# Gated attention on one core: where TensorE's early code is aligned, the rings of the first loads, and the last column block

## The chip, the core and the metric

The kernel runs on one core of a Trainium2 chip. A core has five engines with an instruction stream each: TensorE (PE), which multiplies 128x128 weight tiles with up to 512 columns; VectorE (DVE); ScalarE (ACT); GpSimd (POOL); and SyncE (SP), which here only issues DMA transfers. ACT and POOL can issue transfers as well; each issuing engine has a ring of its own. Engines wait for each other through semaphores. The metric is the device time of one execution in microseconds (us).

## What is computed

```python
xn = layernorm(x)                                # x: 2048 x 640
q  = xn @ wq                                     # 32 heads of 128
s  = concat(softmax(q k^T / sqrt(128)) v) @ wo   # the last 512 keys of the cache
g  = silu(relu(xn @ w1 + b1)**2 @ w2 + b2)       # 640 -> 1728 -> 640
return x + s * g
```

All in float32. A matmul operand is split in a high and a low part (`hi`, `lo` in the names), and one product becomes three matmuls: hi x hi, hi x lo, lo x hi.

## The kernel before

The 2048 rows of x are four tiles of 512 columns once transposed (D on the partitions, five blocks of 128). The work is laid out by hand in one long stream for each engine; `Ordered` (line 69) keeps the engines' instructions in the order in which they are written.

1. **The head**, `ln_first` (226). The first tile's x comes as four blocks of 128 rows. Block 0 is halved between SP's and ACT's rings; blocks 1 and 3 are issued by SP, block 2 by ACT (lines 239 to 243). In the meantime TensorE turns the identity `WARM` times (`pw`, 250). DVE takes the statistics block by block, ACT and POOL make the root, ACT scales blocks 0 and 1, DVE blocks 2 and 3, and TensorE turns them by transposes (`px`). ACT and DVE split the result into `xT`, hi and lo.
2. **The MLP of tiles 0 to 2**, `mlp_step` (471), one call a step over `steps`, 14 chunks of the hidden dimension for each tile. Step n does the up-projection of chunk n (`up`, 414, psum `ph`; relu, square and split follow on ACT, POOL and DVE) and then the down-projection of chunk n - 1 (`down`, 442, five psums `py`). A whole chunk is 15 matmuls up and 15 down; the chunk of 64 rows has 10 and 10. Weights are loaded and split on the way in tile 0. In one step of each tile a transpose of the next tile's layer norm statistics stands behind the up-projection (`ln_rows`, 176).
3. **Attention**, 128 units in a fixed period, planned by times in a list `plan` and sorted (lines 986 to 1181): scores, maximum, exponent, values, output projection into `acc`. The MLP of the last tile is spread over the end of it (`late_up`, `late_down`).
4. **The end.** `late_down` fills the psums `ly` one column block after the other, and `late_gate` (925) finishes each: ACT's silu into a tile `lsg` in SBUF, DVE's product with the attention's result `acc`, DVE's sum with x (`lx`), and a store issued by SP. The last block, d = 4, is done in two halves of 256 columns: both silus, then product, sum and store of the first half, then those of the second.

`pe.addr_align(BLOCK, slot)` fills TensorE's instruction stream with NOPs until the next instruction stands at `slot`, counted modulo `BLOCK` = 256 instructions. It is called at the beginning of the warm-up with `LEAD_SLOT` = 88 (line 249), and five times in each attention unit (`align`, 1021), at `FIRST_SLOT` = 188 plus 128 for odd units plus an offset of `SLOTS`. Between line 249 and the first unit there is none.

Of the kernel before, what the change touches and what calls it, by code (L numbers as in the profile page):

```python
# [8 lines left out]
F32 = mybir.dt.float32  # L9
F32R = mybir.dt.float32r  # L10
AF = mybir.ActivationFunctionType
ALU = mybir.AluOpType
AX = mybir.AxisListType

P = 128
NT = 512
EPS = 1e-5
WARM = 40
BLOCK = 256
FIRST_SLOT = 188  # L20
SLOTS = (0, 11, 22, 33, 42)
LEAD_SLOT = 88


@with_exitstack
def kernel(
# [20 lines left out]
    DC = D // P  # L47
# [3 lines left out]
    LN_AT = {t: (3, 7) if t == LATE else (5, 9) for t in range(1, NTILE)}  # L51
    SCALE = DH**-0.5
    G = 2
    HALF = 2
# [8 lines left out]
    b1_sb, b2_sb = b_sb[:, :FC], b_sb[:, FC : FC + DC]  # L63
    chunks = [(f0, min(P, F - f0)) for f0 in range(0, F, P)]
# [4 lines left out]
    class Ordered:  # L69
# [13 lines left out]
    pe, dve, act, pool, sp = (  # L83
        Ordered(e) for e in (nc.tensor, nc.vector, nc.scalar, nc.gpsimd, nc.sync)
    )
# [8 lines left out]
    def raw(ap):  # L94
        return ap.bitcast(F32)
# [39 lines left out]
    def ln_tile(t, b):  # L135
        tag = "stage" if b < 2 else "mr"
        return xp.tile([P, D], F32, tag=tag, name=f"xb{t}_{b}")
# [3 lines left out]
    def ln_load(t):  # L141
        mv = xp.tile([P, 4, NB], F32, tag="mv", name=f"mv{t}")[:, :2, :]
        sc = xp.tile([P, 3, NB], F32, tag="sc", name=f"sc{t}")
        xn = []
        for b in range(NB):
            xb = ln_tile(t, b)
            r0 = t * NT + b * P
            nc.sync.dma_start(xb, x[r0 : r0 + P, :])
            xn.append(xb)
        LS[t] = mv, sc, xn  # L150

    def ln_block(t, b):
        mv, sc, xn = LS[t]
        st = xp.tile([P, 2, 6], F32, tag="st", name=f"st{t}_{b}", bufs=4)
        hd = D // 2
        for i in range(2):
            dve.bn_stats(st[:, i, :], xn[b][:, i * hd : (i + 1) * hd])
        dve.bn_aggr(mv[:, :, b], st)

    def ln_var(t):  # L160
        mv, sc, xn = LS[t]
        dve.tensor_scalar(sc[:, 0, :], mv[:, 1, :], EPS, None, op0=ALU.add)
        nc.scalar.activation(sc[:, 1, :], sc[:, 0, :], AF.Sqrt)

    def ln_root(t):
        mv, sc, xn = LS.pop(t)
        var, sd, y = (sc[:, i, :] for i in range(3))
        r = mv[:, 1, :]
        dve.reciprocal(y, sd)
        dve.tensor_tensor(r, y, y, op=ALU.mult)  # L170
        dve.tensor_tensor(r, r, var, op=ALU.mult)
        dve.tensor_scalar(r, r, -0.5, 1.5, op0=ALU.mult, op1=ALU.add)
        dve.tensor_tensor(r, r, y, op=ALU.mult)
        return mv
# [21 lines left out]
    def ln_chunk(t, bc, xs, c):  # L196
        xc = xp.tile([P, D], F32, tag="stage", name=f"xc{t}_{c}")[:, :NT]
        nc.sync.dma_start(xc, xT[c * P : (c + 1) * P, t * NT : (t + 1) * NT])
        dve.tensor_tensor(xc, xc, bc[0], op=ALU.subtract)
        nc.vector.tensor_tensor(xc, xc, bc[1], op=ALU.mult)  # L200
        nc.scalar.activation(xs[0][:, c, :], xc, AF.Copy)
        nc.vector.tensor_tensor(xs[1][:, c, :], xc, raw(xs[0][:, c, :]), op=ALU.subtract)
# [23 lines left out]
    def ln_first():  # L226
# [3 lines left out]
        n = NB // 2  # L230
# [7 lines left out]
        xn = [ln_tile(0, b) for b in range(NB)]  # L238
        for i, q in enumerate((sp, act)):
            js = slice(i * hd, (i + 1) * hd)  # L240
            q.dma_start(xn[0][:, js], x[:P, js])
        for b in range(1, NB):
            (sp if b % 2 else act).dma_start(xn[b], x[b * P : (b + 1) * P, :])
        act.activation(warm, warm, AF.Sqrt)
        br = xp.tile([P, P], F32, tag="br", name="br", bufs=1)
        dve.memset(br, 0.0)
        BR.append(br)
        pw = psx.tile([P, NT], F32, tag="x", name="pw")
        pe.addr_align(BLOCK, LEAD_SLOT)
        for _ in range(WARM):  # L250
            pe.transpose(pw[:, :P], ident, ident)
        pts = [ps_y.tile([P, NT], F32, tag="py", name=f"px0_{c}") for c in range(DC)]
        xs = [
            xp.tile([P, DC, NT], F32R, tag=f"xT{i}", name=f"xT0_{i}", bufs=1) for i in range(2)
        ]
# [59 lines left out]
        for cs in (range(2), range(2, DC)):  # L315
            js = slice(cs[0] * P, (cs[-1] + 1) * P)
            for b in range(n, NB):
                m, q = mv[:, 0, b : b + 1], mv[:, 1, b : b + 1]
# [17 lines left out]
    def spill(t, xs, cs=slice(0, DC)):  # L336
        for i in range(2):
            pool.dma_start(xT_d[t][i][:, cs, :], raw(xs[i])[:, cs, :])

    def load_part(f, k, held=False):  # L340
        f0, n = chunks[f]
        if f % 3 and f < 9:
            if k == 0:
                BOTH[f] = keep.tile([P, 2, D], F32, tag="acc", name=f"wr{f}", bufs=2)
            w = BOTH[f][:, k, :]
        else:
            w = xp.tile([P, D], F32, tag="stw", name=f"w{k + 1}r{f}", bufs=2)
            if held:
                dve.memset(w[:, :1], 0.0)
        if k == 0:  # L350
            w = w.rearrange("p (c n) -> p c n", n=P)[:, :, :n]
            sp.dma_start(w, w1[:, f0 : f0 + n].rearrange("(c p) f -> p c f", p=P))
        else:
            for i in range(0, P, n):
                sp.dma_start(w[i : i + n, :], w2[f0 : f0 + n, :])
        PRE[f, k] = w
# [14 lines left out]
    def split_w(f, k):  # L371
        if f < FC:
            split_hi(f, PRE[f, k], k)
            split_lo(f, PRE[f, k], k, dve)
            if 9 <= f < FC - 1:
                load_part(f + 1, k)
# [81 lines left out]
    steps = [(t, f) for t in range(LATE) for f in range(FC)]  # L458
    XS, HS, PY, LN = {0: xs_next}, {}, {}, {}

    def gate(t, tiles):
        for d in range(DC):
# [5 lines left out]
            )  # L468
            nc.gpsimd.dma_start(g_d[t][:, d, :], sg)

    def mlp_step(n):
        if n < len(steps):
            t, f = steps[n]
            ln_stats_at, ln_chunk_at = LN_AT[t + 1]
            if t == 0 and f == 1:
                ln_load(1)
            if t == 0 and f == 6:
                LN[1] = ln_root(1)
            if t and f == ln_stats_at - 1:
                ln_load(t + 1)  # L480
            if t and f == ln_stats_at:
                for b in range(NB):
                    ln_block(t + 1, b)
                ln_var(t + 1)
                LN[t + 1] = ln_root(t + 1)
            c = f - ln_chunk_at
            if 0 <= c < DC:
                ln_chunk(t + 1, *LN[t + 1], c)
                XS[t + 1] = LN[t + 1][1]
            if t + 1 == LATE and 0 < c <= DC:  # L490
                spill(t + 1, XS[t + 1], slice(c - 1, c))
            if t == 0 and f > 0:
                split_w(f, 1)
                if f < 8:
                    for k in range(2):
                        load_part(f + 2, k)
            HS[n] = up(t, f, XS[t])
            if t == 0 and 2 <= f < 2 + NB:
                ln_block(1, f - 2)
                if f == NB + 1:  # L500
                    ln_var(1)
            if f == ln_stats_at + 2:
                LN[t + 1] = ln_rows(t + 1, LN[t + 1])
            if t > 0 and f == 1:
                spill(t - 1, XS[t - 1])
            if t == LATE - 1 and f == 3:
                spill(t, XS[t])
        if n > 0:
            t, f = steps[n - 1]
            if f == 0:  # L510
                PY[t] = [
                    ps_y.tile([P, NT], F32, tag="py", name=f"py{t}_{d}") for d in range(DC)
                ]
            down(t, f, HS.pop(n - 1), PY[t])
            if f == FC - 1 and t < LATE - 1:
                gate(
                    t,
                    lambda d: xp.tile(
                        [P, D], F32, tag=("stage", "mr")[d % 2], name=f"sg{t}_{d}"
                    )[:, :NT],  # L520
                )


    TPH = NTILE // HALF
# [251 lines left out]
    def store(q, hf, t, d, a, j=slice(0, NT)):  # L776
        t0 = (hf * TPH + t) * NT
        q.dma_start(outT[d * P : (d + 1) * P, t0 + j.start : t0 + j.stop], a[:, j])

    LW, LH, LPH, LPY, LR = {}, {}, {}, {}, {}  # L780
# [143 lines left out]

    def late_gate(d):
        py, a = LPY[d], ACC[HALF - 1, TPH - 1][:, d, :]
        sg = ap.tile([P, NT], F32, tag=("bm", "bs")[d % 2], name=f"lsg{d}", bufs=2)
        k = 2 if d == DC - 1 else 1
        js = [slice(i * NT // k, (i + 1) * NT // k) for i in range(k)]
        for j in js:  # L930
            act.activation(sg[:, j], py[:, j], AF.Silu, bias=b2_sb[:, d : d + 1])
        for j in js:
            dve.tensor_tensor(a[:, j], sg[:, j], a[:, j], op=ALU.mult)
            dve.tensor_tensor(a[:, j], a[:, j], LR["x"][:, d, j], op=ALU.add)
            store(sp, HALF - 1, TPH - 1, d, a, j)

    steps_n = len(steps)
    opened = (LATE - 1) * FC + FO
# [40 lines left out]
    ap = ctx.enter_context(tc.tile_pool(name="at", bufs=2))  # L979
# [122 lines left out]
    for item in order:  # L1102
        kind, n = item[0], int(item[1:] or 0)
# [125 lines left out]
```

## Time and profile before

| | us |
|---|---|
| median of 3 runs | 1960.47 (1960.15 to 1961.4) |
| the profiled execution | 1961.36 |
| its span, first to last instruction | 1959.6 |
| TensorE busy in it | 1951.1 |

The profile is of one execution. Its views: the page (busy time of each engine, the chain of work that ended last, groups of instructions); busy time by stretches of time, where each engine has its busy us and, as (xN), its number of instructions, followed by TensorE's granted clock, the share of the DMA engines and GB/s; the order in time, with start, duration, engine, line, operation, output<-input, shapes, number, and in brackets the idle time ahead and what ended it; the instructions of one line, with count, shortest/median/longest duration in ns and first and last start in us; and the chain of waits. PEld are weight loads, which run beside matmuls; a name with q (SPq, PEldq) is an instruction that the engine's sequencer handles, such as an issue, a wait or a NOP. Most instructions that go through the wrapper have line 77, so tiles tell them apart.

### The profile page before, as it was taken

To read this page: it belongs to the slowest core of one execution; us is meant where nothing else is said; L and a number is where in the kernel's file an instruction comes from. 1 tells how busy PE (TensorE), PEld (TensorE's weight loads), DVE (VectorE), ACT (ScalarE), POOL (GpSimd) and SP (SyncE) were. 2 spreads that over 40 slices of the span, in tenths; PEclk is the share of its full clock that TensorE was granted. 3 is DMA by queue.
4 is the path that set the end of the run, shared out by engine and by line. 5 is a ranking of instruction groups with operands and counts; after the bars stand their busy time and mean duration, and the time that the engine had idled before them with its cause. 6 is when DMAs were issued, how large, how long until landed. Compare 5 with 4: busy or idle time off the path is not lost.

```text
span 1959.6 us, 28181 instructions
## 1 busy us (share of the span) xinstructions
PE 1951.1 (100%) x8616; PEld 1611.8 (82%) x8616; DVE 1534.8 (78%) x2638; ACT 1187.1 (61%) x2039; POOL 1375.7 (70%) x757
## 2 busy tenths in 40 slices
PE   9999999999999999999999999999999999999998
PEld 7888888888888888888888888888888888888887
DVE  5633337788888888888888878888888888888865
ACT  4432336766666666666666676666666666666643
POOL 2121226888888888888887888888888888888841
PEclk9999999999999999999999999999999999999999
DMA  5330454333333232223335433443333333333353
GB/s 182 94 119 28 183 198 128 98 93 92 92 92 92 92 92 93 92 92 93 92 92 174 145 119 108 114 114 114 113 114 114 114 114 114 98 92 92 85 189 118
DMA packets 127892, 219.13 MB, mean 112 GB/s; under 512 B 23452, under 2 KB 38086, under 8 KB 126470
## 3 DMA queue, kind: packets, MB, share of 16 engines
q1 hardware_dynamic: 124598, 202.43, 34.1%
q0 software_dynamic: 2864, 14.42, 1.8%
q8 instruction: 77, 1.26, 0.2%
q14 instruction: 65, 0.53, 0.1%
q10 hardware_dynamic: 288, 0.49, 0.1%
HBM read 193.41 MB, written 23.87 MB: 111 GB/s over the span
## 4 chain that ended last, share of the span: by engine, by line
PE 98%; DMA 1%; DVE 1%; POOL 0%; ACT 0%; issue 0%; SPq 0%; POOLq 0%; ACTq 0%
PE r L77 22%; PE pq L77 22%; PE o L77 18%; PE s L77 18%; PE ph L425 7%; PE ly L77 2%; PE py L101 2%; PE py L100 2%; PE py L102 2%; PE lu L77 2%; PE eu L77 0%; PE ph L396 0%; POOL pt L77 0%; DMA xb<-in_x_dram 0%; PE py L448 0%; PE py L447 0%
## 5 line engine op out<-in xcount | busy, mean ns | idle before, releaser
L77 POOL TENSOR_TENSOR pt<-e,pt 128x1024 fp32r<-128x1024 f32 x256 | 615.5, 2404 | 115.2 <-ACT pt L77 69.1
L77 PE MATMUL r<-ot,wo 128*128 128x512 f32 x1920 | 496.6, 389 | 0.0
L77 PE MATMUL pq<-ax,wq 128*128 128x512 f32 x1920 | 456.1, 389 | 0.0
L77 PEld LDWEIGHTS pq<-ax,wq 128*128 128x128 f32 x1920 | 360.3, 188 | 75.3 <-DVE q L77 0.4
L77 PEld LDWEIGHTS r<-ot,wo 128*128 128x128 f32 x1920 | 360.4, 188 | 74.9
L77 PE MATMUL o<-pt,wv 128*128 128x512 f32 x1536 | 369.7, 389 | 0.1
L77 PE MATMUL s<-q,wk 128*128 128x512 f32 x1536 | 369.1, 389 | 0.1
L77 DVE TRANSPOSE_TENSOR_REDUCE rdm<-s 128x16 f32<-128x512 f32 x512 | 346.5, 711 | 6.2 <-PE s L77 6.0
L77 ACT ACTIVATE e<-e 128x1024 f32<-128x1024 f32 x256 | 269.8, 1054 | 125.5 <-DVE e L77 82.0
L77 PEld LDWEIGHTS o<-pt,wv 128*128 128x128 f32 x1536 | 288.1, 188 | 60.9 <-POOL pt L77 1.2
L77 PEld LDWEIGHTS s<-q,wk 128*128 128x128 f32 x1536 | 288.1, 188 | 60.5 <-DVE e L77 0.7
L77 DVE TENSOR_TENSOR e<-s,bm 128x512 f32<-128x512 f32 x512 | 312.2, 664 | 7.6 <-DMA bm<-m_d 7.1
L77 POOL TENSOR_TENSOR su<-e,e 128x1024 f32<-128x1024 f32 x128 | 309.1, 2415 | 0.0
L77 ACT ACTIVATE pt<-e 128x1024 fp32r<-128x1024 f32 x256 | 272.0, 1063 | 6.9
L77 DVE TENSOR_TENSOR acc<-r,acc 128x512 f32<-128x512 f32 x300 | 203.4, 678 | 12.9 <-PE r L77 12.6
L77 ACT ACTIVATE rdm<-rdm 32x64 f32<-32x64 f32 x384 | 97.8, 255 | 181.5 <-DVE rdm L77 178.4
L77 DVE TRANSPOSE_TENSOR_REDUCE rds<-su 128x32 f32<-128x1024 f32 x128 | 158.3, 1237 | 0.3 <-POOL su L77 0.3
L77 DVE TENSOR_TENSOR ot<-o,ot 128x512 fp32r<-128x512 f32 x128 | 88.5, 691 | 86.1 <-ACT ot L77 86.1
L77 ACT ACTIVATE q<-pq 128x512 fp32r<-128x512 f32 x128 | 76.7, 600 | 111.5 <-PE pq L77 111.4
L425 PE MATMUL ph<-xT,w1s 128*128 128x512 f32 x585 | 139.5, 390 | 0.0
L425 PEld LDWEIGHTS ph<-xT,w1s 128*128 128x128 f32 x585 | 109.5, 188 | 23.5 <-DVE xT L77 0.9
L77 ACT ACTIVATE rds<-rds 32x32 f32<-32x32 f32 x384 | 89.7, 234 | 63.0 <-DVE rds L77 59.7
(137 smaller groups left out, 1940.9 us busy)
## 6 DMA issues: line engine op xcount, KB each, us to landing
bm<-m_d SPq DMA_DIRECT2D x128, 256.0 KB, 3.2
bs<-s_d SPq DMA_DIRECT2D x128, 256.0 KB, 4.0
qr<-in_wq_dram SPq DMA_DIRECT2D x64, 320.0 KB, 4.5
or<-in_wo_dram SPq DMA_DIRECT2D x64, 320.0 KB, 4.7
kr<-in_kT_dram SPq DMA_DIRECT2D x64, 256.0 KB, 4.3
vr<-in_v_dram SPq DMA_DIRECT2D x64, 256.0 KB, 4.4
xT_d<-xT POOLq DMA_DIRECT2D x6, 1280.0 KB, 8.0
ax<-xT_d SPq DMA_DIRECT2D x4, 1280.0 KB, 10.6
```

What stands on the lines that cost most here:

```text
L77: ins = method(*args, **kwargs)
L100: nc.tensor.matmul(ps, ah, bh, start=first and i == 0, stop=False)
L101: nc.tensor.matmul(ps, ah, bl, start=False, stop=False)
L102: nc.tensor.matmul(ps, al, bh, start=False, stop=last and i == n - 1)
L425: nc.tensor.matmul(ph, w1s[f][i][:, c, :], xs[j][:, c, :], start=k == 0, stop=k == len(order) - 1,)
```

## The change

There are three edits.

- **The early aligns.** The align ahead of the warm-up goes, and `WARM` falls from 40 to 38. In `mlp_step`, between the up-projection of step n and the down-projection of step n - 1, an align is set for n = 1 to 23. Its slot comes from a new function `lead_slot`: a base of 171, plus two instructions for each matmul of the steps so far (`ups`, `downs`), two for each transpose of statistics (`turns`), plus two for each step.
- **The first loads.** Blocks 1 to 3 of the first x are all issued by SP, one behind the other; ACT issues its half of block 0 alone.
- **The last column block.** For d = 4 the silus write back into the psum `ly`. The first half's product goes to `acc` by DVE, POOL adds x to it, and ACT issues its store. The second half's product stays in the psum, DVE adds x into `acc`, and SP issues its store. The two stores are issued after all the arithmetic in the program. Blocks 0 to 3 are as before.

```diff
-WARM = 40
+WARM = 38
-LEAD_SLOT = 88
+LEAD_SLOTS, LEAD_PADS = 171, 2
...
         for b in range(1, NB):
-            (sp if b % 2 else act).dma_start(xn[b], x[b * P : (b + 1) * P, :])
+            sp.dma_start(xn[b], x[b * P : (b + 1) * P, :])
...
-        pe.addr_align(BLOCK, LEAD_SLOT)
         for _ in range(WARM):
             pe.transpose(pw[:, :P], ident, ident)
...
+    LEAD_N = 23
+
+    def lead_slot(n):
+        ups = sum(2 * (2 if chunks[steps[k][1]][1] < P else 3) * DC for k in range(n + 1))
+        downs = sum(2 * (2 if chunks[steps[k][1]][1] < P else 3) * DC for k in range(n - 1))
+        turns = 2 * sum(1 for k in range(n + 1) if steps[k][1] == LN_AT[steps[k][0] + 1][0] + 2)
+        return (LEAD_SLOTS + ups + downs + turns + LEAD_PADS * n) % BLOCK
...
+            if 0 < n <= LEAD_N:
+                pe.addr_align(BLOCK, lead_slot(n))
...
     def late_gate(d):
         py, a = LPY[d], ACC[HALF - 1, TPH - 1][:, d, :]
-        sg = ap.tile([P, NT], F32, tag=("bm", "bs")[d % 2], name=f"lsg{d}", bufs=2)
-        k = 2 if d == DC - 1 else 1
-        js = [slice(i * NT // k, (i + 1) * NT // k) for i in range(k)]
+        xs, b2 = LR["x"][:, d, :], b2_sb[:, d : d + 1]
+        if d < DC - 1:
...
+            return
+        js = [slice(i * NT // 2, (i + 1) * NT // 2) for i in range(2)]
         for j in js:
-            act.activation(sg[:, j], py[:, j], AF.Silu, bias=b2_sb[:, d : d + 1])
-        for j in js:
-            dve.tensor_tensor(a[:, j], sg[:, j], a[:, j], op=ALU.mult)
-            dve.tensor_tensor(a[:, j], a[:, j], LR["x"][:, d, j], op=ALU.add)
-            store(sp, HALF - 1, TPH - 1, d, a, j)
+            act.activation(py[:, j], py[:, j], AF.Silu, bias=b2)
+        dve.tensor_tensor(a[:, js[0]], py[:, js[0]], a[:, js[0]], op=ALU.mult)
+        pool.tensor_tensor(a[:, js[0]], a[:, js[0]], xs[:, js[0]], op=ALU.add)
+        dve.tensor_tensor(py[:, js[1]], py[:, js[1]], a[:, js[1]], op=ALU.mult)
+        dve.tensor_tensor(a[:, js[1]], py[:, js[1]], xs[:, js[1]], op=ALU.add)
+        for j, q in zip(js, (act, sp)):
+            store(q, HALF - 1, TPH - 1, d, a, j)
```

More of the change, by code (lines that the diff above doesn't have):

```diff
@@ L926, in late_gate @@
         py, a = LPY[d], ACC[HALF - 1, TPH - 1][:, d, :]
-        sg = ap.tile([P, NT], F32, tag=("bm", "bs")[d % 2], name=f"lsg{d}", bufs=2)
-        k = 2 if d == DC - 1 else 1
-        js = [slice(i * NT // k, (i + 1) * NT // k) for i in range(k)]
-        for j in js:
-            act.activation(sg[:, j], py[:, j], AF.Silu, bias=b2_sb[:, d : d + 1])
-        for j in js:
-            dve.tensor_tensor(a[:, j], sg[:, j], a[:, j], op=ALU.mult)
-            dve.tensor_tensor(a[:, j], a[:, j], LR["x"][:, d, j], op=ALU.add)
-            store(sp, HALF - 1, TPH - 1, d, a, j)
+        xs, b2 = LR["x"][:, d, :], b2_sb[:, d : d + 1]
+        if d < DC - 1:
+            sg = ap.tile([P, NT], F32, tag=("bm", "bs")[d % 2], name=f"lsg{d}", bufs=2)
+            act.activation(sg, py, AF.Silu, bias=b2)
+            dve.tensor_tensor(a, sg, a, op=ALU.mult)
+            dve.tensor_tensor(a, a, xs, op=ALU.add)
+            store(sp, HALF - 1, TPH - 1, d, a)
+            return
+        js = [slice(i * NT // 2, (i + 1) * NT // 2) for i in range(2)]
+        for j in js:
+            act.activation(py[:, j], py[:, j], AF.Silu, bias=b2)
[5 more added lines that the diff above has]
+            store(q, HALF - 1, TPH - 1, d, a, j)
     steps_n = len(steps)
```

## The prediction, made before the result was known

> **What bounds the kernel now.** I read the page first, then busy time by stage, then the chain of waits at both ends.
>
> ```profile
> PE 1951.1 (100%) x8616; PEld 1611.8 (82%) x8616; DVE 1534.8 (78%) x2638; ACT 1187.1 (61%) x2039; POOL 1375.7 (70%) x757
> PE 98%; DMA 1%; DVE 1%; POOL 0%; ACT 0%; issue 0%; SPq 0%; POOLq 0%; ACTq 0%
> ```
>
> ```profile
> 12.40:20.00 7.60, 7.60 (x34) 5.66 (x33) 4.95 (x9) 4.57 (x9) 3.85 (x3) 1.00 0.72 238
> 20.00:296.00 276.00, 275.96 (x1218) 226.95 (x1217) 109.11 (x188) 97.20 (x150) 56.84 (x67) 1.00 0.36 125
> ...
> 315.00:1954.50 1639.50, 1639.23 (x7226) 1355.03 (x7224) 1399.58 (x2394) 1067.80 (x1854) 1306.11 (x664) 1.00 0.36 107
> 1954.50:1959.60 5.10, 0.00 (x0) 0.00 (x0) 1.61 (x4) 0.84 (x2) 0.00 (x0) 0.94 0.28 103
> ```
>
> TensorE is the bound. From 20 to 296 us it starts 1218 matmuls in 276.0 us, 0.2266 us each; from 315 to 1954.5 it is 0.2269. No stage in between has anything to gain, and whatever stops TensorE there is paid in full. What can be won lies ahead of 20 us and behind 1954.5 us. What can be lost lies wherever TensorE's own instruction stream gets longer.
>
> **The new aligns: how much filler each puts in.** An align fills TensorE's stream with NOPs up to a slot, counted modulo 256 instructions. The old one stands ahead of the warm-up and asks for slot 88. These are the NOPs of the first 2.6 us, the identity's last instruction, and TensorE's first two groups:
>
> ```profile
> L77 PEldq NOP  x23: 13/13/13, 0.8 to 2.5; - x23
> ```
>
> ```profile
> 1.03 0.29 POOL masks.py:199 TENSOR_SCALAR_AFFINE_SELECT ident<-ident 128x128 f32<-128x128 f32 x1
> ```
>
> ```profile
> 2.55 6.51 PE L77 MATMUL pw<-ident 128*128 128x128 f32 x40 [2.55 <-issue]
> 9.39 3.29 PE L77 MATMUL px<-ident,xb 128*128 128x128 f32 x20 [0.33 <-ACT xb L77]
> ```
>
> 23 NOPs reach slot 88, so the kernel's stream begins at slot 88 - 23 = 65. I test this way of counting on the next align, which asks for slot 188 after 1324 matmuls (counted in the program's order). A matmul is two instructions, a weight load and a multiply (8616 of each on the page). The stream also holds separate semaphore waits. Up to 296 us the rows of lines 77, 100 and 425 show
>
> ```profile
> L77 PEldq EVENT_SEMAPHORE  x6: 51/51/51, 7.0 to 285.5; - x6
> ```
>
> ```profile
> L100 PEldq EVENT_SEMAPHORE  x3: 51/51/51, 16.4 to 203.6; - x3
> ```
>
> ```profile
> L425 PEldq EVENT_SEMAPHORE  x1: 51/51/51, 37.9 to 37.9; - x1
> ```
>
> 88 + 2 x 1324 + 10 = 2746, which is slot 186 of its block: 2 NOPs are due. The trace, 290 to 297 us:
>
> ```profile
> L77 PEldq NOP  x2: 13/13/13, 295.7 to 295.7; - x2
> ```
>
> So the count holds. Now the changed stream. Its first align stands behind the second up-projection and ahead of the first down-projection. Before it come 38 warm-up and 20 turning transposes, 15 + 1 + 15 matmuls (first up, biases, second up), in all 89, and the waits up to 16.4 us:
>
> ```profile
> L77 PEldq EVENT_SEMAPHORE  x5: 51/51/51, 7.0 to 14.8; - x5
> ```
>
> It stands at 65 + 2 x 89 + 5 = 248. It asks for LEAD_SLOTS + 60 (two ups of 15 matmuls) + 2 (pads) = 171 + 62 = 233. That is 15 slots *behind* it, so the filler runs around the block: 256 - 15 = **241 NOPs**. The other 22 new aligns, counted the same way, need 1 or 2 each, 41 in all; the main part's first needs 3 where it needed 2. NOPs in all: 2528 - 23 + 241 + 41 + 1 = 2788.
>
> **What 241 NOPs cost.** NOPs go one by one through TensorE's sequencer. 23 take from 0.8 to 2.5 us (ends 0.75 and 2.52 by the neighbours, 0.077 each at most), and eight between 333.6 and 334.3 us take
>
> ```profile
> L77 PEldq NOP  x8: 13/13/13, 333.7 to 334.2; - x8
> ```
>
> 0.5 us over seven steps, 0.071 each. I take 0.073, since long runs lean to neither end: 241 x 0.073 = 17.6 us (17.1 to 18.6). Part of it is covered, for the sequencer runs ahead of the array. The wait that stands where the new align will stand, and what the array had begun by then:
>
> ```profile
> L100 PEldq EVENT_SEMAPHORE  x1: 51/51/51, 16.4 to 16.4; - x1
> ```
>
> ```profile
> 0.00:16.43 16.43, 13.35 (x76) 11.14 (x77) 11.12 (x32) 9.50 (x16) 4.82 (x14) 1.00 0.85 284
> ```
>
> At 16.43 us 76 of 91 matmuls had started: a lead of 15, about 3.4 us. Small fills vanish in that lead (the eight above did), and the 41 do too. The long one does not. What waits behind it is TensorE's whole stream, the first down-projection first:
>
> ```profile
> 15.36 4.81 PE L425 MATMUL ph<-xT,w1s 128*128 128x512 f32 x20
> 20.00 0.39 PE L100 MATMUL py<-h,w2s 128*128 128x512 f32 x1
> 20.44 0.50 PE L101 MATMUL py<-h,w2s 128*128 128x512 f32 x1
> 20.77 0.40 PE L102 MATMUL py<-h,w2s 128*128 128x512 f32 x1
> ```
>
> With the head 0.88 us earlier (below) the fill begins at 16.43 - 0.88 = 15.55, ends at 33.15, and the first `py` runs at about 33.4 instead of 20.00: **+13.4**. The steps 20.00, 20.44, 20.77 hold 0.31 us of waiting for `h` above two pitches of 0.23; `h` will be long done: **-0.3**.
>
> The array then idles some 14 us, and its clock falls. At the end of the trace the mean granted clock of the last 5.10 us is 0.94: if it halves, it did so 0.6 us before the end, about 4.5 us after the last matmul. How long it takes to come back is seen in the warm-up, by stretches:
>
> ```profile
> 0.00:6.50 6.50, 3.95 (x19) 3.98 (x20) 1.00 0.63 216
> 6.60:9.06 2.46, 2.46 (x23) 2.22 (x21) 1.00 0.91 272
> ```
>
> 19 transposes in 3.95 us, 0.208 each, then 23 in 2.46, 0.107 each: half speed for 4.0 us. Four microseconds at half speed after the fill lose **+2.0** (0 if the clock stays, 4 if it takes twice as long). [...]
>
> Can the aligns gain anything? In 20 to 296 us the pitch is 0.2266 and the best row of any stage is no lower, so at most some tenths. [...] I put it at 0.
>
> **The head.** Without the 23 NOPs the warm-up may begin when the identity is done, 1.03 + 0.29 = 1.32, not 2.55. That wins nothing by itself: it ended at 9.06, and the turning waits for ACT's scaling until 9.39. 38 instead of 40 end earlier still, and the pause, under 2 us, is below the 4.5 us. The path is x:
>
> ```profile
> 1.19 4.34 DMA xb<-in_x_dram
> ```
>
> ```profile
> 4.62 0.06 DVE L77 MEMSET w1r<- 128x1 f32 x1
> 5.56 0.89 DVE L77 BATCH_NORM_STATS2 st<-xb 128x6 f32<-128x320 f32 x2 [0.88 <-DMA xb<-in_x_dram]
> ...
> 6.80 0.49 DVE L77 BATCH_NORM_STATS2 st<-xb 128x6 f32<-128x320 f32 x1
> ...
> 7.91 0.83 DVE L77 BATCH_NORM_STATS2 st<-xb 128x6 f32<-128x320 f32 x2
> ```
>
> Block 1, issued at 1.19, is usable at 5.54, while block 2 comes beside it on ACT's ring. With block 2 behind it on the same ring, block 1 gets the engines alone, and DVE can go on at 4.68: **-0.88**, and all up to the fill moves with it. Lower bound of the gain is 0 (both share the same engines anyhow). If every block takes its turn and block 3, now fourth of the ring, comes after 7.03, up to 0.5 is lost. I take the gain: there are 1.2 us of room for blocks 2 and 3 each behind block 1.
>
> **The tail.**
>
> ```profile
> 1954.53 0.84 ACT L77 ACTIVATE lsg<-ly,b_sb 128x256 f32<-128x256 f32 x2 [2.03 <-PE ly L77]
> 1955.03 0.42 DVE L77 TENSOR_TENSOR acc<-lsg,acc 128x256 f32<-128x256 f32 x1 [1.08 <-ACT lsg L77]
> 1955.49 0.43 DVE L77 TENSOR_TENSOR acc<-acc,lx 128x256 f32<-128x256 f32 x1
> 1955.84 0.42 DVE L77 TENSOR_TENSOR acc<-lsg,acc 128x256 f32<-128x256 f32 x1
> 1956.29 0.42 DVE L77 TENSOR_TENSOR acc<-acc,lx 128x256 f32<-128x256 f32 x1
> ```
>
> ```profile
> DMA to landing us min/median/max: 1.9/1.9/2.2
> ```
>
> ```profile
> 1902.09 1.04 POOL L77 TENSOR_TENSOR lr<-lr 128x512 f32<-128x512 f32 x1 [10.87 <-ACT lr L77]
> ```
>
> DVE loses the first add: product two at 1955.44, add two to about 1956.31, SP's store 0.4 us sooner. POOL's add of 256 columns is not in the trace: between half of the 512-column square (0.52) and all of it (1.04), I take 0.6: 1955.5 to 1956.1, then ACT's issue, landing near 1958.1, just ahead of SP's 1958.2. **-0.4**; with the slow end, or a slow start of a ring idle since the head, up to +0.4.
>
> **Sum.** 13.4 - 0.3 + 2.0 - 0.4 = +14.7 us, the head inside the 13.4. The profiled execution took 1961.36 us around its span of 1959.6; it becomes 1976.1. The median of the timed runs, 1960.47, lies 0.9 below: **1975.2 us**.
>
> **The rivals.** *The fill is short* (0.19; not slower). The start slot of 65 comes from one profiled execution. What stands ahead of the kernel's stream isn't the kernel's, and a timed execution may carry another length of it. The point that decides is 50: from 45 to 50 the first fill is 5 to 0 NOPs and hidden in the lead; from 51 on it wraps to 241 to 255. Then head and tail remain: 1960.47 - 0.88 - 0.4 = 1959.2 us, within 0.2% of before. For it speaks only that no row here is of a timed execution. Against it: from slot 48, say, the old fill would be 40 NOPs or 2.9 us, the old warm-up would end about 10.3 instead of 9.06, past the 9.39 at which x is ready, and timed executions would be some 0.9 us longer than the profiled one; they are 0.9 us shorter. *The fill is long but cheap* (inside the forecast's range): the clock stays up, 1973.2. *Head and tail turn against the change and the fill is short*: +0.5 and +0.4 give 1961.4, still within 0.2%.
>
> **How the numbers follow.** The long fill has 0.80, the short 0.19, a gain past 0.2% that I can't name 0.01. 0.2%, about 3.9 us, is what a measurement here can tell from no change. The range is the long fill's, which leaves out the other 0.2: low, NOPs at 0.071 (-0.5) and no cold clock (-2.0), 1972.7, set at 1972.5; high, NOPs at 0.077 (+1.0), a longer cold stretch (+2.0), no gain at the head (+0.9), rounded down since they hardly all meet, 1978.5. So slower 0.80, same 0.19, faster 0.01.
>
> **What would show it.** NOP x2788, with 241 in one run from about 15.5 to 33 us; TensorE idle from 19 to 33 and then matmuls twice as far apart for 4 us; DVE's wait for block 1 gone; SP's last store at 1956.3 less the shift of the rest. If the run of NOPs is 2 long, the forecast falls whole; if it is 241 long and TensorE waits less than 12 us, my pace of a NOP is wrong.

## The result and the profile after

The changed kernel takes **1976.34 us** (median of six runs, 1975.57 to 1977.54), the kernel before 1961.12 (six runs, 1960.15 to 1961.5): a ratio of 1.0079, interval 1.0066 to 1.0092, or 15.2 us more. The profiled execution took 1975.57 us around a span of 1973.8 us, 14.2 us more than the one before. Forecast: 1975.2 us, range 1972.5 to 1978.5.

The page of the changed kernel, first the busy times, then TensorE's slices and clock, then the chain:

```profile
PE 1951.8 (99%) x8614; PEld 1613.3 (82%) x8614; DVE 1536.5 (78%) x2637; ACT 1186.9 (60%) x2039; POOL 1374.8 (70%) x758
...
PE   6999999999999999999999999999999999999998
...
PEclk8999999999999999999999999999999999999999
...
PE 98%; issue 1%; ACT 0%; DMA 0%; DVE 0%; POOL 0%; SPq 0%; POOLq 0%
```

TensorE's busy time is the old one. What is new is a first slice (49 us) that is 6 tenths busy, with a clock of 8 tenths, and 1% of the chain under "issue": time in which TensorE waits for nothing that the profile names. The NOPs of the whole execution, then those from 12 to 36 us:

```profile
L77 PEldq NOP  x2788: 13/13/13, 15.5 to 1868.7; - x200
```

```profile
L77 PEldq NOP  x241: 13/13/13, 15.5 to 33.3; - x121
```

Both counts are those forecast. 241 NOPs take 17.8 us, 0.074 us each. TensorE meanwhile, in the timeline:

```profile
14.48 4.81 PE L424 MATMUL ph<-xT,w1s 128*128 128x512 f32 x20
33.51 0.77 PE L100 MATMUL py<-h,w2s 128*128 128x512 f32 x1 [14.21 <-issue]
34.07 0.63 PE L101 MATMUL py<-h,w2s 128*128 128x512 f32 x1
34.49 0.63 PE L102 MATMUL py<-h,w2s 128*128 128x512 f32 x1
34.92 0.63 PE L100 MATMUL py<-h,w2s 128*128 128x512 f32 x1
```

The first down-projection starts at 33.51 instead of 20.00, after 14.21 us without a matmul, and then the matmuls stand 0.427 apart where 0.227 is the pace. Short stretches on both sides of the places where the clock changes; behind the core's busy times the column PEclk is the granted clock:

```profile
22.50:23.16 0.66, 0.00 (x0) 0.00 (x0) 0.66 (x2) 0.00 (x0) 0.00 (x0) 1.00 1.14 387
23.16:24.00 0.84, 0.00 (x0) 0.00 (x0) 0.14 (x1) 0.00 (x0) 0.00 (x0) 0.50 0.63 246
36.00:36.81 0.81, 0.81 (x3) 0.62 (x3) 0.00 (x0) 0.00 (x0) 0.00 (x0) 0.50 0.00 0
36.81:37.50 0.69, 0.69 (x5) 0.56 (x4) 0.00 (x0) 0.00 (x0) 0.00 (x0) 1.00 0.00 0
```

The clock halved at 23.16, 3.9 us after the last matmul's end (19.29), and was back at 36.81, 3.3 us after the first `py`. In the head, DVE's stream:

```profile
4.40 0.21 DVE L77 BATCH_NORM_AGGREGATE mv<-st 128x2 f32<-128x12 f32 x1
4.54 0.49 DVE L77 BATCH_NORM_STATS2 st<-xb 128x6 f32<-128x320 f32 x1
...
5.92 0.49 DVE L77 BATCH_NORM_STATS2 st<-xb 128x6 f32<-128x320 f32 x1
```

The wait of 0.88 us for block 1 is gone: its statistics begin at 4.54 instead of 5.56. The tail, in the timeline of all engines, and the landings of the last stores from their issue:

```profile
1968.16 0.93 ACT L77 ACTIVATE ly<-ly,b_sb 128x256 f32<-128x256 f32 x2 [2.03 <-PE ly L77]
1969.12 0.42 DVE L77 TENSOR_TENSOR acc<-ly,acc 128x256 f32<-128x256 f32 x1 [1.54 <-ACT ly L77]
1969.58 0.43 DVE L77 TENSOR_TENSOR ly<-ly,acc 128x256 f32<-128x256 f32 x1
1969.63 0.72 POOL L77 TENSOR_TENSOR acc<-acc,lx 128x256 f32<-128x256 f32 x1 [26.36 <-DVE acc L77]
1970.05 0.42 DVE L77 TENSOR_TENSOR acc<-ly,lx 128x256 f32<-128x256 f32 x1
1970.38 0.38 ACTq L77 DMA_DIRECT2D out_dram<-acc  x1
```

```profile
DMA to landing us min/median/max: 1.9/2.2/2.2
```

The first product starts 0.96 us after the first silu (before: 0.50), and the last sum ends 2.31 us after it (before: 2.18), with one add less on DVE. POOL's add takes 0.72 us. Of the last two stores ACT's lands 1.95 us and SP's 2.22 us after its issue.

**Where the 14.2 us are.** The starts of the same matmuls in both traces give a ledger, after minus before, added up along the way:

| place | difference, us |
|---|---|
| first turning transpose (8.51 for 9.39) | -0.88 |
| first `py` (33.51 for 20.00) | +13.5 |
| 15th `py`, full clock again | +14.8 |
| last matmul | +13.6 |
| end of the span | +14.2 |

Between the 15th `py` and the last matmul 1.2 us are given back. These are TensorE's waits in the attention stages, 310 to 1940 us, of the kernel before and then of the changed one:

```profile
PEld o L77 <- POOL pt L77: 1.2, 3, 0.5
PEld s L77 <- DVE e L77: 0.7, 2, 0.6
```

```profile
PEld o L77 <- POOL pt L77: 0.5, 2, 0.3
```

A third wait, 0.4 us, is the same in both. No line of the change touches that work, and the stretch differs as much between the profiles of the experiments below: from the 15th `py` to the last matmul e2, f1, f2, f4, g1 and g2 take 1929.2 to 1929.6 us, as the changed kernel (1929.4), and e1, e3, e4, f3 and g3 1930.0 to 1930.6, as the kernel before (1930.6). So this is variation, not a gain. Without it the ledger would end at +15.4; the medians say +15.2.

### The profile page after: what moved, and what is told of

The parts are those of the page before. It is cut to its first block, busy times and chain, and to the rows that moved or that the text cites. A ratio compares the mean times of both kernels' runs of the same rounds, so it can differ in the third digit from the quotient of the medians.

```text
span 1973.8 us, 28438 instructions
## 1 busy us (share of the span) xinstructions
PE 1951.8 (99%) x8614; PEld 1613.3 (82%) x8614; DVE 1536.5 (78%) x2637; ACT 1186.9 (60%) x2039; POOL 1374.8 (70%) x758
## 4 chain that ended last, share of the span: by engine, by line
PE 98%; issue 1%; ACT 0%; DMA 0%; DVE 0%; POOL 0%; SPq 0%; POOLq 0%
PE pq L77 22%; PE r L77 22%; PE o L77 18%; PE s L77 18%; PE ph L424 6%; PE ly L77 2%; PE py L100 2%; PE py L101 2%; PE py L102 2%; PE lu L77 2%; PE eu L77 1%; PE ph L395 0%; DMA xb<-in_x_dram 0%; PE py L447 0%; PE py L446 0%
```

## The experiments

**The theory**: nearly all of the loss is the one fill of 241 NOPs, as far as it is longer than the sequencer's lead, and the cold clock behind it. The other aligns, the ring and the new tail move less than 1 us each. **Rivals**: the number of NOPs or aligns costs, wherever they stand; or the tail or the ring has a share in the loss.

**e1: the changed kernel with a shorter warm-up, so that the first align is met by 1 NOP.**

```diff
-WARM = 38
+WARM = 30
```

> The changed kernel with WARM = 30 instead of 38: 16 instructions fewer ahead of the first new align, so that it stands at slot 232 and needs 1 NOP instead of 241; all else of the change stays. Theory (one long run of NOPs holds TensorE): the loss goes away whole. The head stays 0.88 us early (first px at 8.5, first py at about 19.1 us) and the tail keeps the 0.55 us that the changed kernel's profile shows it to be longer than before, so about 1961.1 - 0.9 + 0.55 = 1960.8 us. Rival (the other 22 aligns, the ring or the tail carry the loss): it stays near 1976 us.

Measured: 1960.25 us against 1960.62, ratio 0.9999 (0.9991 to 1.0008). The NOPs from 10 to 20 us, then TensorE's timeline:

```profile
L77 PEldq NOP  x1: 13/13/13, 15.6 to 15.6; - x1
```

```profile
14.50 4.79 PE L424 MATMUL ph<-xT,w1s 128*128 128x512 f32 x20
19.13 0.39 PE L100 MATMUL py<-h,w2s 128*128 128x512 f32 x1
```

With all 23 aligns, the ring and the new tail still in place, the whole loss is gone. The first `py` comes 0.87 us before that of the kernel before. In this execution a wait of DVE for a block of x takes that back (215 to 232 us): `h` comes late, and from 224.85 to 226.21 no matmul starts, 1.1 us more than the pace.

```profile
DVE st L77 <- DMA xb<-in_x_dram: 4.4, 1, 4.4
```

```profile
226.21 0.50 PE L446 MATMUL py<-h,w2s 128*128 128x512 f32 x1 [0.97 <-DVE h L386]
```

Gaps of 0.84 to 1.03 us between two starts at the same place show in the profiles of e3, e4 and f3 below, and none in the others. In the attention the kernel before then waits longer, as said above, so that at the last matmul e1 is 0.87 us ahead again, and at the end 0.33: the head's -0.87 and the tail's +0.54.

**e2: the kernel before with the fill alone**: an align at step 1 that needs 241 NOPs, and one at step 20 that restores the old slots.

```diff
+FILL = {1: 4, 20: 100}
...
+            if n in FILL:
+                pe.addr_align(BLOCK, FILL[n])
```

> The kernel before with nothing added but a run of 241 NOPs at the place of the changed kernel's first align (and 15 NOPs later, at step 20, so that the attention's aligns stand where they stood). Theory: NOPs from 16.4 to 34.1 us, first py at 34.4 instead of 20.0 (+14.4), 0.3 us of waiting for h saved, 1.8 us lost to the clock: +15.9 us, about 1977.0. Rival (part of the loss is the new head or tail, or the clock's state there): clearly less than +14 us.

Measured: 1976.58 us against 1960.62, ratio 1.0083 (1.0069 to 1.0097). The NOPs from 9 to 60 us, the first `py`, and the clock on both sides of its return:

```profile
L78 PEldq NOP  x241: 13/13/13, 16.7 to 34.3; - x121
```

```profile
34.45 0.77 PE L101 MATMUL py<-h,w2s 128*128 128x512 f32 x1 [14.00 <-issue]
```

```profile
22.50:23.24 0.74, 0.00 (x0) 0.00 (x0) 0.73 (x2) 0.74 (x2) 0.00 (x0) 1.00 0.49 102
23.25:24.00 0.75, 0.00 (x0) 0.00 (x0) 0.75 (x2) 0.34 (x1) 0.00 (x0) 0.50 1.14 342
39.50:40.31 0.81, 0.81 (x3) 0.62 (x3) 0.00 (x0) 0.00 (x0) 0.00 (x0) 0.50 0.00 0
40.32:41.00 0.68, 0.68 (x5) 0.56 (x4) 0.00 (x0) 0.00 (x0) 0.00 (x0) 1.00 0.00 0
```

The fill alone makes the whole loss and more: first `py` +14.45, and +16.9 when the clock is back. In the profiles the one edit costs more than all together for two reasons: without the other edits the first `py` comes 0.95 us later than in the changed kernel, and the array then stays at half speed for 5.9 us (34.45 to 40.31), against 3.3 there. Behind the attention the span is 15.6 us longer than that of the kernel before.

**e3: the kernel before with as many NOPs in seven short runs**: 40 at step 1, and 36 each at steps 6, 10, 14, 18, 22 and 26, 256 in all.

```diff
+FILL = {1: 59, 6: 121, 10: 143, 14: 163, 18: 174, 22: 186, 26: 206}
...
+            if n in FILL:
+                pe.addr_align(BLOCK, FILL[n])
```

> The kernel before with 256 NOPs more, but in seven runs: 40 at step 1 and 36 each at steps 6, 10, 14, 18, 22 and 26. Theory (a run costs only what exceeds the sequencer's lead of about 3.4 us, some 46 NOPs): every run is hidden, 1961.1 us within 0.5. Rival (each NOP costs its 0.073 us wherever it stands): +18.7 us, about 1979.8.

Measured: 1960.03 us against 1960.62, ratio 0.9999 (0.999 to 1.0008). The first two runs, from 9 to 60 us, and the first `py`:

```profile
L78 PEldq NOP  x76: 13/13/13, 16.5 to 50.8; - x76
```

```profile
20.06 0.39 PE L101 MATMUL py<-h,w2s 128*128 128x512 f32 x1
```

256 NOPs cost nothing that the times can show when each run (at most 40 NOPs, 3.0 us at 0.074) fits in the lead. It is not the NOPs or the aligns that cost, it is the length of one run.

**e4: the kernel before with a run of 100 NOPs** at step 1, and four of 39 later.

```diff
+FILL = {1: 119, 8: 50, 14: 193, 20: 61, 26: 206}
...
+            if n in FILL:
+                pe.addr_align(BLOCK, FILL[n])
```

> The kernel before with a run of 100 NOPs at step 1 and four hidden ones of 39 at steps 8, 14, 20 and 26. Theory: NOPs from 16.4 to 23.75, first py at 24.05 instead of 20.0, less 0.3 us of waiting for h: +3.75 us, 1964.9, if the array's clock outlasts an idle time of 3.9 us; with another 1.0 to 1.8 us, about 1966.4, if it does not. Rival (no cover by the lead): +7.3 us and the clock on top, 1969 or more.

Measured: 1966.23 us against 1960.62, ratio 1.0031 (1.0019 to 1.0042). The first run, the first `py`, and the clock around its fall:

```profile
L78 PEldq NOP  x100: 13/13/13, 16.3 to 23.6; - x100
```

```profile
23.76 0.53 PE L101 MATMUL py<-h,w2s 128*128 128x512 f32 x1 [3.75 <-ACT w2s L78]
```

```profile
23.00:24.02 1.02, 0.26 (x1) 0.29 (x2) 1.02 (x2) 0.17 (x1) 0.00 (x0) 1.00 1.13 380
24.03:25.00 0.97, 0.97 (x4) 0.71 (x3) 0.00 (x0) 0.00 (x0) 0.00 (x0) 0.50 0.33 129
```

Of 7.3 us of NOPs 3.76 show, so 3.5 are covered by the lead. The releaser that the timeline infers (`w2s`) isn't the cause: the run of NOPs ends at 23.6. The clock still fell, 0.26 us *after* the matmuls had begun again, and cost another 1.3 us (+5.1 when it was back, at 27.44).

**f1: the ring alone, in the kernel before.**

```diff
         for b in range(1, NB):
-            (sp if b % 2 else act).dma_start(xn[b], x[b * P : (b + 1) * P, :])
+            sp.dma_start(xn[b], x[b * P : (b + 1) * P, :])
```

> The kernel before with block 2 of the first x issued by SP (the ring edit alone). Theory: block 1 is usable 0.88 us sooner, as in the changed kernel; the warm-up with its 23 NOPs ahead still ends about 9.0, so the first px comes at 8.9 rather than 8.51, but the second block's at 9.4, and the first py is 0.8 to 0.88 us earlier, at 19.15. In the end about -0.9 us, give or take the 1 us by which stalls on loads differ from one execution to the next. Rival (it takes the early start of the warm-up as well): the first py gains 0.4 or less.

Measured: 1960.4 us against 1960.59, ratio 0.9999 (0.999 to 1.0008). The first `py` stands at 19.51, 0.49 us earlier, between theory and rival. Its line, and what is missing in DVE's timeline:

```profile
19.51 0.39 PE L100 MATMUL py<-h,w2s 128*128 128x512 f32 x1
```

```profile
6.29 0.49 DVE L77 BATCH_NORM_STATS2 st<-xb 128x6 f32<-128x320 f32 x1 [0.43 <-DMA xb<-in_x_dram]
```

Block 1 is on time here too, but now DVE waits 0.43 us for a later block, which the changed kernel's profile did not (5.92). All profiles without a long fill, by the start of their first `py`, tell how far that varies:

| loads of the first x | first `py`, us | mean |
|---|---|---|
| both rings (before, e3, f2, f3, g1) | 20.00, 20.06, 19.84, 20.48, 19.63 | 20.00 |
| one ring (e1, f1, f4, g2, g3) | 19.13, 19.51, 19.45, 19.70, 19.59 | 19.48 |

In the profiles the ring is worth about 0.5 us. f1, which has the late warm-up, stands in the middle of the others of its row, so the early warm-up adds nothing that these profiles can tell. The medians of the timed runs leave it open: f1 lies 0.2 us below the kernel before, and g2 below, which has the same tail and the early warm-up as well, 0.7.

**f2: the new last block alone, in the kernel before** (the third edit of the change, nothing else).

```diff
-            act.activation(sg[:, j], py[:, j], AF.Silu, bias=b2_sb[:, d : d + 1])
+            act.activation(py[:, j], py[:, j], AF.Silu, bias=b2)
...
+        pool.tensor_tensor(a[:, js[0]], a[:, js[0]], xs[:, js[0]], op=ALU.add)
```

> The kernel before with the new last column block alone. Theory (the two silus, now in place in one psum, go one after the other, and the first product waits for both; and the two stores meet on the same DMA engines): from the last matmul to the end 6.0 us instead of 5.5, so +0.55 us. Rival (the tail of the forecast; what the changed kernel shows comes from its long fill): -0.4 us, 5.1.

Measured: 1960.48 us against 1960.59, ratio 1.0 (0.9991 to 1.0009). From the start of the last matmul to the end of the span it takes 6.02 us, as the changed kernel (6.03) and e1 (6.02); the kernel before, e2, e3, e4 and f1 take 5.48 or 5.49. So the new tail costs 0.54 us by itself; the medians, whose intervals reach 0.09% to either side, are too coarse to show it. The timeline repeats that of the changed kernel:

```profile
1952.99 0.93 ACT L77 ACTIVATE ly<-ly,b_sb 128x256 f32<-128x256 f32 x2 [2.03 <-PE ly L77]
1953.95 0.42 DVE L77 TENSOR_TENSOR acc<-ly,acc 128x256 f32<-128x256 f32 x1 [1.54 <-ACT ly L77]
```

**f3: the new tail with the silus in SBUF again**, as they were, so that they overlap; products and sums stay in SBUF, POOL's add and ACT's store stay.

```diff
-            act.activation(py[:, j], py[:, j], AF.Silu, bias=b2)
+            act.activation(sg[:, j], py[:, j], AF.Silu, bias=b2)
...
-        dve.tensor_tensor(py[:, js[1]], py[:, js[1]], a[:, js[1]], op=ALU.mult)
-        dve.tensor_tensor(a[:, js[1]], py[:, js[1]], xs[:, js[1]], op=ALU.add)
+        dve.tensor_tensor(a[:, js[1]], sg[:, js[1]], a[:, js[1]], op=ALU.mult)
+        dve.tensor_tensor(a[:, js[1]], a[:, js[1]], xs[:, js[1]], op=ALU.add)
```

> The kernel before with the new last column block, but the silus go to the SBUF tile as before, so that they overlap and the first product waits for the first alone; POOL adds x to the first half and ACT issues its store, as in the change. Theory: the last sum ends 1.85 us after the first silu starts (2.18 before, 2.31 in the changed kernel), but the two stores are issued within 0.15 us and the second one's packets wait some 0.3 us for the first one's, so from the last matmul to the end 5.4 us, within 0.1 of before. Rival (only the order of the silus costs, the stores don't meet): 5.1 us.

Measured: 1960.87 us against 1960.59, ratio 1.0001 (0.9992 to 1.0009). The tail takes 5.71 us: better than 6.02, worse than the old 5.48, and neither of the two that I had expected.

```profile
1954.44 0.84 ACT L77 ACTIVATE lsg<-ly,b_sb 128x256 f32<-128x256 f32 x2 [2.03 <-PE ly L77]
1954.94 0.79 DVE L77 TENSOR_TENSOR acc<-lsg,acc 128x256 f32<-128x256 f32 x2 [1.08 <-ACT lsg L77]
1955.45 0.87 POOL L77 TENSOR_TENSOR acc<-acc,lx 128x256 f32<-128x256 f32 x1 [26.40 <-DVE acc L77]
1955.77 0.83 DVE L77 TENSOR_TENSOR acc<-acc,lx 128x256 f32<-128x256 f32 x1
```

The first product follows its silu after 0.50 us again, 0.46 earlier than in f2. But DVE's last add now takes 0.83 us instead of 0.42, and POOL's beside it 0.87 instead of 0.72: both read two operands in SBUF. So the last sum ends only 0.15 us earlier against the first silu than in f2 (2.16 for 2.31). The stores are now issued 0.28 us apart, and SP's lands 2.02 us after its issue, 0.2 sooner than in f2.

**g1: as f3, but the second product goes to the psum**, so that DVE's last sum has one operand there.

```diff
-        dve.tensor_tensor(a[:, js[1]], sg[:, js[1]], a[:, js[1]], op=ALU.mult)
-        dve.tensor_tensor(a[:, js[1]], a[:, js[1]], xs[:, js[1]], op=ALU.add)
+        dve.tensor_tensor(py[:, js[1]], sg[:, js[1]], a[:, js[1]], op=ALU.mult)
+        dve.tensor_tensor(a[:, js[1]], py[:, js[1]], xs[:, js[1]], op=ALU.add)
```

> The kernel before with a third form of the last column block: silus to the SBUF tile (they overlap), the second product into the psum, so that DVE's last sum has one SBUF input while POOL adds. Theory (three terms: silus one after the other 0.46, two adds on the same SBUF 0.40, two stores that meet 0.3): only the meeting stores remain; the last sum ends 1.75 us after the first silu starts (2.18 before), SP issues at 1.78, lands 2.2 later, so from the last matmul to the end 5.4 to 5.5 us, no better than 5.48 before. Rival (the stores cost nothing by meeting): 5.1 us.

Measured: 1960.63 us against 1960.43, ratio 1.0001 (0.9993 to 1.001). The tail again takes 5.71 us, for another reason:

```profile
1952.80 0.84 ACT L77 ACTIVATE lsg<-ly,b_sb 128x256 f32<-128x256 f32 x2 [2.03 <-PE ly L77]
...
1953.82 0.87 POOL L77 TENSOR_TENSOR acc<-acc,lx 128x256 f32<-128x256 f32 x1 [26.40 <-DVE acc L77]
1954.14 0.42 DVE L77 TENSOR_TENSOR acc<-ly,lx 128x256 f32<-128x256 f32 x1
1954.60 0.33 SPq L77 DMA_DIRECT2D out_dram<-acc  x1
1954.71 0.35 ACTq L77 DMA_DIRECT2D out_dram<-acc  x1
```

DVE's sum is back at 0.42 us and ends 1.76 us after the first silu's start, 0.42 earlier than in the old tail. Now POOL's add is last (0.87 us, beside DVE's product of two SBUF operands), and its store, issued 0.11 us after SP's, ends the kernel: it lands 2.15 us after its issue, SP's 1.88. The span ends 1.22 us behind that landing, where it was 0.97 in the kernel before; no run shows why.

**f4, g2, g3: the change without its early aligns** (`LEAD_N = 0`), with three tails: that of f3 (f4), the old one (g2), that of g1 (g3). The align ahead of the attention then needs 29 NOPs in one run.

```diff
-    LEAD_N = 23
+    LEAD_N = 0
```

> The changed kernel without its 23 early aligns (the first align is then the attention's, with 29 NOPs in one run) and with the last block of the run before this one. Theory: 29 NOPs, 2.1 us, hide in the lead of 17 matmuls, 3.9 us; first px at 8.5, first py at 19.1, tail 5.4: some 0.9 us under the kernel before, give or take 1 us of stalls on loads. Rival (the early aligns are worth something): stalls of TensorE between 20 and 300 us that the kernel before and the run with WARM = 30 do not have.

> The changed kernel without its 23 early aligns and with the last block as it was before: the ring edit and the early warm-up alone. Theory: first py at 19.1 to 19.5, tail 5.48, so 0.6 to 0.9 us under the kernel before in the profile's path, some tenths more than the run with the overlapping silus and two SBUF adds (tail 5.71). Rival (the early start does not last): no difference from before.

> The run before this one with the third form of the last block. Theory: the same within 0.1 us from the last matmul to the end (5.4 to 5.5). Rival (stores do not meet): 0.35 us less.

| kernel | median, us | before, us | ratio (interval) | tail, us |
|---|---|---|---|---|
| f4 | 1959.71 | 1960.59 | 0.9996 (0.9987 to 1.0005) | 5.71 |
| g2 | 1959.74 | 1960.43 | 0.9995 (0.9986 to 1.0004) | 5.48 |
| g3 | 1959.91 | 1960.43 | 0.9997 (0.9988 to 1.0006) | 5.71 |

The 29 NOPs, 2.1 us at 0.074 each, are shorter than the lead of 3.4 us, and the medians show no loss. Without the 23 early aligns the stages up to 296 us show no idle time that they had not with them, so these aligns gain nothing that the profiles can show. All three are 0.5 to 0.9 us below the kernel before, and every interval holds 1: no version here is shown to beat it.

## Why the prediction was right, and where it was not

- **The count of the filler** held: 241 NOPs in one run, 2788 in all. e1 turns on the same count: eight transposes fewer (16 instructions) bring the stream to slot 232, and the fill falls from 241 to 1, as counted.
- **The pace and the lead** held: 0.074 us for a NOP where 0.073 was taken, and first `py` at 33.51 for 33.4. e4 gives the lead a second time: 3.5 us covered, where 3.4 had been read from 15 matmuls.
- **The cold clock** was a little oversized. From the first to the 15th `py` the loss grew by 1.3 us; with the 0.3 of saved waiting that is 1.6, for 2.0. The array was at half speed for 3.3 us, not 4.0. e2 (5.9 us) and e4 (3.4 us) show that no single size is right, so that 2.0 came near 1.6 is partly luck. (The prediction's 0.208 and 0.107 us for a transpose count some of them twice; the starts stand 0.213 and 0.109 apart, and its 4.0 us hold.) Nor is its 4.5 us of idle time a limit: the clock fell 3.9 us after the last matmul's end here, and in e4 after an idle time of 3.75 us.
- **The head**: the -0.88 came, wholly, in the profiled execution, and in e1. Over ten profiles it is about -0.5: sometimes DVE then waits for a later block.
- **The tail was wrong**, in sign: -0.4 forecast, +0.55 measured. The step that failed says that DVE "loses the first add" and all behind it moves up. Three things took its place. The silus in place in one psum go one after the other (the pair takes 0.93 us, for 0.84), and the first product waits for both, not for its own half, so it starts 0.46 us later. In the trace the second silu carries a wait on the semaphore that ACT's own instructions raise, and it starts 0.03 us after the first one's end; into SBUF it carries none and starts 0.10 us before that end. So the order is one that the program asks for; whether ACT would overlap the halves of one psum without it, no run shows. Next, the two stores are issued 0.12 us apart and SP's lands 2.2 us after its issue, for 1.9 before, where they had been 0.8 apart. In the DMA records the second store's first packet starts 1.11 us after the issue, for 0.84 before, and the whole store starts 0.34 us behind the first one. And POOL's add is 0.72, not 0.6. Of the 0.55 us, 0.13 lie in the arithmetic (2.31 for 2.18) and about 0.3 in the landing; some 0.1 behind it I can't place.
- **The aligns' own gain** of 0 held (f4, g2, g3 against e1).
- **The rivals**: the short fill did not happen, in any of the executions; its time, had it happened, is nearly what e1 shows (1960.25 for 1959.2, the tail being the difference). "Long but cheap" fell with the clock. Head and tail did pull in different directions, each by half a microsecond.

The sum was +14.7 and the profile has +14.2, of which -1.2 is the slow attention in the profile of the kernel before. So the sum was about 0.7 us short of the path: the tail (0.95 us) and the first `py` (0.1), less the 0.4 by which the cold clock was oversized. That the profile came so near to the sum is luck; the medians (+15.2) show the miss.

## What to carry to other kernels

An align in a long instruction stream fills modulo its block: here a target 15 slots behind the stream cost 241 of the block's 256 instructions. So count the slot, from a measured run of filler, for every align. A run of NOPs cost only what exceeded the sequencer's lead (here 3.4 to 3.5 us, about 47 NOPs), so 256 of them in seven runs cost nothing measurable while 241 in one cost 14.5 us and then the clock. Handing the last bits of a tail to a second engine and a second ring won nothing by itself here (tails of 5.71 to 6.02 us, for 5.48): halves worked in place in one buffer went one after the other (0.93 us for the pair, for 0.84), adds of two engines on SBUF took longer side by side (0.83 and 0.87 us, for 0.42 and 0.72), and of two stores issued 0.12 us apart the later one landed late (2.22 us after its issue, for 1.9).

## What the hardware showed that I had not expected

**The clock's changes lie whole steps apart.** In the changed kernel's trace it changes at 6.09 (end of the cold warm-up), 23.16 and 36.81 us: 17.07 and 13.65 us apart, five and four times 3.413. In e2 the changes at 6.18, 23.25 and 40.31 are five and five such steps apart, in e4 those at 6.96, 24.02 and 27.44 five and one. The first and the last change lie 572 steps apart in the profile of the kernel before (6.57 and 1959.00 us) and 576 in that of the changed kernel (6.09 and 1972.17). The sizes above fit this. In the changed kernel a step ends at 33.40, just ahead of the first `py` (33.51), and the clock is back at the end of the next. In e2 one ends at 33.49 and the first `py` is 0.96 us behind it; the step after it, with matmuls in 72% of it, ended at half clock, and at the end of the next one, at 40.31, the clock was back. In e4 the step from 20.61 to 24.02 was idle but for its last 0.26 us, and the clock fell while matmuls ran. So some 14 us of idle cost 1.6 us in one profile and 2.8 in another, which fits where the steps lay. The timed runs of e4 spread over 3.1 us (1964.92 to 1968.06), those of the kernel before beside them over 1.7, as this would have it. At the ends of the profiles the clock fell 4.5 us after the last matmul's end in the kernel before and 4.0 us after it in the changed one: the step in which that matmul ended, with matmuls in 68 and 81% of it, ended at full clock, and the fall came at the end of the idle one behind it. Where the warm-up begins at 2.55 us, its 40 transposes take 6.32 us in e2, 6.51 in the kernel before, 6.70 in e4 and 7.12 in e3; by its starts, 0.213 us apart ahead of the change and 0.109 behind it, the clock was up at 6.18, 6.57, 6.96 and 7.82 us.

**Two adds on SBUF took longer side by side**: 128x256 f32 adds of DVE and POOL side by side took 0.83 and 0.87 us (f3), where DVE alone takes 0.42 and POOL, beside a DVE add that reads the psum, 0.72 (the changed kernel). In g1, where one operand of DVE's sum lies in the psum, that sum is back at 0.42 us. Not every overlap shows it: DVE's product that was already running when POOL began took no longer than alone (0.43). In f3 and f4 DVE's add ends 0.28 us after POOL's, so it may wait for POOL to be done rather than run slower beside it; no run tells the two apart.
